# Polysketch attention into a SwiGLU block: key sums of the third batch in steps, two matmul groups one unit later, one subtraction on another engine

## The chip, the cores and the metric

One core of a Trainium2 chip runs the whole program in one launch. The metric is the device time of that launch in microseconds, given as the median of the runs shown. Each core has TensorE (PE; its weight loads are PEld), VectorE (DVE), ScalarE (ACT), GpSimd (POOL) and SyncE (SP); instructions of one engine run in the order in which they are issued, and engines wait for each other by semaphores. DMA transfers are issued from the queues of SP, ACT and POOL.

## The reference

```python
def phi(x):                                   # x: (4, 4, 1088, 32), S1 and S2: (8, 32)
    a = einsum('rd,bhsd->bhsr', S1, x)
    b = einsum('rd,bhsd->bhsr', S2, x)
    return einsum('bhsi,bhsj->bhsij', a, b).reshape(..., 64)
q_p, k_p = phi(q), phi(k)
kv  = einsum('bhsf,bhsd->bhfd', k_p, v)
z   = sum(k_p, axis=2)
num = einsum('bhsf,bhfd->bhsd', q_p, kv)
den = einsum('bhsf,bhf->bhs', q_p, z)[..., None] + 1e-06
x   = (num / den) as (4352 tokens, 128)
out = (silu(x @ w_gate) * (x @ w_val)) @ w_out    # 128 -> 1536 -> 128
```

Batches are numbered 0 to 3 in the code; "the third batch" of the title is the last one, `b = 3`.

## The kernel before

The SwiGLU block is most of the work. Its 4352 tokens are cut into blocks: three for batch 0 (of 384, 320 and 384 tokens) and seven of up to 480 tokens for the rest (`line` holds these seven, blocks 3 to 9). The hidden width of 1536 is cut into 12 chunks of 128. The last phase of the kernel is one loop over `y` from 0 to 83 (lines 1396 to 1411): unit `y` is chunk `y % 12` of block `3 + y // 12`.

One unit (`fine_unit`, line 1003) makes six matmuls (line 1012): gate and value product, each of three matmuls on parts of the numbers (x1, x0, xd against three parts of the weights). ACT takes the silu (line 1017), DVE multiplies (line 1026) and writes the hidden chunk h into a slot of `hbuf`. Each unit's two products take a pair of PSUM banks, of which there are three; the pair is free again when line 1026 has read it. Each h is cut into three parts too (`cut_hidden`, line 966): ACT makes h1 (line 983), DVE makes h0 one unit later (line 990), and hd, the sum of h and h1 (which has the opposite sign), is made either on DVE (line 994) or, for the chunks of blocks 3 to 5 but for three and for every second chunk of blocks 6 to 8, by two DMAs: SP copies h into hd (line 980), and POOL then issues a DMA that adds h1 into hd (line 985). Six units later, after `fine_unit`, `down` (line 1072) makes the three matmuls of that chunk with `w_out` (line 1084), with h1, h0 and hd in this order. Tiles for these parts come from a free list (`h_more`, line 915): rooms of earlier tiles join it from a given unit on.

The parts of a block's tokens are made ahead by `cut_tokens` (line 877): x1 on ACT (line 885) and the difference xd (line 894), then x0 on DVE (line 888), then its scaling on ACT (line 902). The loop at lines 1391 to 1395 says in which units each step is issued; block 5 (m = 2), used from unit 24, has units 20, 21 and 22.

The attention of batches 1 to 3 runs between these units. It is a Python generator (`attentions`, line 624) that stops at each `yield`. After a unit, `parts_of` (line 1409) lets it go on by one step, in the units that its condition names. A `yield "pe"` marks a group of matmuls; the generator stays there until `group()` is called, ahead of the units in `GROUPS` (line 1387). For batches 2 and 3 the groups are: keys with values and key sums (line 397, then line 724 through `value_sums`), query sketches (line 351), and numerators (line 798). The groups of batch 3 are the ones ahead of units 27, 29 and 44.

Behind the numerators of batch 2 (group ahead of unit 20) the key features of batch 3 are made on DVE, in four products of 3, 2, 2 and 2 chunks of the tile `late` (`features`, line 714; the operation is line 386): the generator stops behind the first, the third and the fourth. Then POOL adds the nine chunks up into `zs`, in five additions (`feature_sums`, line 552, the operation is line 556):

```python
def last():
    add(s[:, 0, :], s[:, 0, :], s[:, 1, :])
    add(s[:, 0, :], s[:, 0, :], rows[:, 8, :])
return s[:, 0, :], [
    lambda: add(s, rows[:, 0:2, :], rows[:, 2:4, :]),
    lambda: add(s, s, rows[:, 4:6, :]),
    lambda: add(s, s, rows[:, 6:8, :]),
    last,
]
```

`value_sums` (line 721) reads `zs` on TensorE into the bank that holds the keys with values; DVE folds that into the query weights (lines 610 to 617) and turns the rest (line 734), and SP sends six small copies of it (`spread`, line 748), one per unit.

Of the kernel before, what the change touches and what calls it, by code (L numbers as in the profile page):

```python
# [19 lines left out]
def kernel(  # L20
# [28 lines left out]
    nc = tc.nc  # L49
# [72 lines left out]
    def pair(keep=None):  # L122

        i = min((i for i in (0, 4, 6) if i not in held), key=lambda i: max(used[i], used[i + 1]))
        touch(i, i + 1)
        if keep is not None:
            held.add(i)
            kept[keep] = i
        return PS[:, i : i + 2, :]
# [3 lines left out]
    def let_go(keep):  # L133
        i = kept.pop(keep)
        held.discard(i)
        touch(i, i + 1)
# [17 lines left out]
    qld = const.tile([P, 4 * NC, Dh], FP32, tag="qld", name="qld", bufs=1)  # L154
    vld = const.tile([P, H, NC, Dh], FP32, tag="vld", name="vld", bufs=1)
    kT = const.tile([P, NC, 4, 32], FP32, tag="kT", name="kT", bufs=1)
    qT = const.tile([P, 4 * NC, 32], FP32, tag="qT", name="qT", bufs=1)
# [160 lines left out]
    late = const.tile([P, NL - NX1, BW], FP32, tag="late", name="late", bufs=1)  # L318
# [40 lines left out]
    def key_products(ps, c0, c1):  # L359

        for c in range(c0, c1):
            for a in (0, 2):
                nc.tensor.matmul(  # L363
                    ps[32 * a : 32 * a + 64, 64 * (c - c0) : 64 * (c - c0) + 64],
                    kT[:, c, a : a + 2, :].rearrange("p a t -> p (a t)"),
                    s12[:].rearrange("p h t r -> p (h t r)"),
                    start=True,
                    stop=True,
                )
# [206 lines left out]
    def turn_keys(b):  # L576

        for c in kpieces:
            turn_k(*c)
            if c[1] == NC and b + 1 < B:  # L580
                load_k(b + 1)
            yield

    def turn_queries(b):

        for x0, x1 in ((0, 4 * kpieces[0][1]), (4 * kpieces[0][1], 4 * NC)):
            nc.vector.transpose(out=qT[:, x0:x1, :], in_=qld[:, x0:x1, :])
            if x1 == 4 * NC and b + 1 < B:
                load_q(b + 1)
            yield  # L590
# [33 lines left out]
    def attentions():  # L624

        yield from turn_keys(1)
        kp = pair("keys")
        for i, c in enumerate(kpieces):  # L630
            key_products(kp[:, i, :], *c)
        ka = apool.tile([P, NC * H, R], FP32, tag="kas", name="kas")

        def sketch(ps, i):
            c0, c1 = kpieces[i]
            return ps[:, i, 0 : 64 * (c1 - c0)].rearrange("p (x t r) -> p x t r", t=2, r=R)

        for i, (c0, c1) in enumerate(kpieces):
            nc.scalar.copy(ka[:, H * c0 : H * c1, :], sketch(kp, i)[:, :, 0, :])
        yield from turn_queries(1)  # L640
        phk = apool.tile([P, NC, H, R, R], FP32, tag="phk", name="phk")
        for n, (i, c0, c1) in enumerate(((0, 0, 3), (0, 3, 5), (1, 5, 7), (1, 7, 9))):
            first = H * (c0 - kpieces[i][0])
            kb = sketch(kp, i)[:, first : first + H * (c1 - c0), 1, :]
            key_features(phk, (ka[:, H * c0 : H * c1, :], kb), c0, c1)
            if n == 0:
                zs, sums = feature_sums(phk)
            else:
                sums.pop(0)()
            if n == 3:  # L650
                let_go("keys")
            if n % 3 != 1:
                yield
        sums.pop(0)()
        yield from turn_keys(2)
        kvz = pair("values")
        key_values(kvz[:, 0, 0:F], phk, 0, NC)
        kab, copies = sketched(pair(), key_products, 2, "kab2")
        run_copies(copies, 2)
        value_sums(kvz[:, 0, :], zs)  # L660
        fold(kvz[:, 0, :])
        spread = spread_out(1, kvz[:, 0, :])
        let_go("values")
        yield
        qab, copies = sketched(pair(), query_sketches, 3, "qab")
        run_copies(copies, 2)
        yield
        yield from query_step(1, qab)
        numerators(1, spread)
        yield "first"  # L670

        phk = apool.tile([P, NC, H, R, R], FP32, tag="phk", name="phk")
        yield from features(phk, kab)
        zs, sums = feature_sums(phk)
        for f in sums:
            f()
        yield from turn_keys(3)
        yield from turn_queries(2)
        for b in (2, 3):
            yield "pe"  # L680
            kv = bank("g2")
            key_values(kv[:, 0:F], phk, 0, NC)
            if b == 2:
                kab, copies = sketched(pair(), key_products, 2, "kab2")
                run_copies(copies, 2)
            value_sums(kv, zs)
            fold(kv)
            spread = spread_out(b, kv)
            yield
            yield "pe"  # L690
            qab, copies = sketched(pair(), query_sketches, 3, "qab")
            run_copies(copies, 2)
            yield
            if b == 2:
                yield from turn_queries(3)
            yield from query_step(b, qab)
            yield "pe"
            numerators(b, spread)
            yield
            if b == 2:  # L700
                phk = late[:].rearrange("p s (n h i j) -> p (s n) h i j", h=1, i=R, j=R)
                phk = phk.rearrange("p (c h) o i j -> p c (h o) i j", h=H)
                yield from features(phk, kab)
                zs, sums = feature_sums(phk)
                for f in sums:
                    f()
                yield

    def run_copies(copies, n):
        for f, *args in copies[:n]:  # L710
# [3 lines left out]
    def features(phk, kab):  # L714
        for n, (c0, c1) in enumerate(((0, 3), (3, 5), (5, 7), (7, 9))):
            x = slice(H * c0, H * c1)
            key_features(phk, (kab[:, 0, x, :], kab[:, 1, x, :]), c0, c1)
            if n % 3 != 1:
                yield
# [157 lines left out]
    def cut_tokens(i, engine=nc.gpsimd):  # L877

        t0, n = blocks[i]
        x = xcols(t0, n)  # L880
        x1, x0, xd = x_parts[i] = [
            apool.tile([P, WB], F32R, tag=tag, name=name, bufs=2)
            for tag, name in (("qb", "x1"), ("dT", "x0"), ("rd", "xd"))
        ]
        nc.scalar.activation(x1[:, 0:n], x, AF.Copy, scale=CUT)

        def low():
            nc.vector.scalar_tensor_tensor(
                out=x0[:, 0:n], in0=whole(x1[:, 0:n]), scalar=-PART, in1=x,
                op0=ALU.mult, op1=ALU.add,  # L890
            )

        def difference():
            engine.tensor_tensor(
                out=xd[:, 0:n], in0=x, in1=whole(x1[:, 0:n]), op=ALU.subtract
            )

        difference()
        yield
        low()  # L900
        yield
        nc.scalar.activation(x0[:, 0:n], whole(x0[:, 0:n]), AF.Copy, scale=LIFT)  # L902
# [11 lines left out]
    h_sets, h_free = {}, []  # L914
    h_more = [
        (1, (("wg", 3), ("wv", 3), ("soon", 3), ("extra", 4), ("xT0", 2))), (6, (("kT", 2), ("kld", 2))),
        (9, (("qld", 2),)), (30, (("vld", 2), ("qT", 2), ("late", 4))),
    ]
    before, behind = {}, {}

# [272 lines left out]
    n = steps[0][1]  # L1193
    pss = query_products(*steps[0], "ab")
    qbs = [query_copy(n, *ps) for ps in pss]
    phk = apool.tile([P, NC, H, R, R], FP32, tag="phk", name="phk")
# [47 lines left out]
    def parts_of(n):  # L1244

        for _ in range(n):
            if ahead[0] not in ("pe", "end"):
                ahead[0] = next(att, "end")
# [135 lines left out]
    slots[:] = [flat[:, WB * k : WB * k + WB] for k in range((NH - NL - NX0) * BW // WB)]  # L1384

    END = len(line) * NCH
    GROUPS = (4, 6, 20, 27, 29, 44)
    LONGER = (18, 42)
    LAG = 6

    token_steps = {}
    for m, i in enumerate(line[1:], 1):
        gen = cut_tokens(i, nc.gpsimd if m < 3 else nc.vector)
        for at in {1: (3, 8, 9), 2: (20, 21, 22), 3: (28, 32, 33), 4: (44, 45, 46)}.get(m, range(NCH * m - 10, NCH * m - 7)):
            token_steps.setdefault(at, []).append(gen)
    for y in range(END):
        if y == NCH * (len(line) - 1):
            rest = apool.tile([P, 6, BW], FP32, tag="phk", name="rest")
            slots += [rest[:, k, :] for k in range(6)]
        if y in GROUPS:  # L1400
            group()
        fine_unit(line[y // NCH], y % NCH, y, mixed=(y == 0))
        if going:
            going.pop(0)()
        for _ in range(2):

            if len(todo) > min(LAG + (y in LONGER), END - y + 1):
                down(y)
        parts_of(y < 30 or y % 2 == 0 or y % 4 == 1)
        for gen in token_steps.get(y, ()):  # L1410
            next(gen, None)
    ps = wide("a")[:, 0, 0:D]
# [42 lines left out]
```

## Time and profile before

| what | value |
|---|---|
| median of 3 runs | 275.98 us (275.47 to 276.18) |
| the profiled execution: its own time | 275.28 us |
| its span, first to last instruction | 273.6 us (1.7 us lie around it) |
| PE busy | 263.9 us, 96% of the span |
| DVE busy | 228.8 us, 84% |
| ACT busy | 147.4 us, 54% |
| POOL busy | 87.4 us, 32% |
| chain that ended last, by engine | PE 85%, DVE 8%, POOL 2%, DMA 2% |
| mean granted TensorE clock | 0.992 |

How to read it: all times in the views are microseconds from the start of the span. A line of the timeline gives the start, the length, the engine, the line of the kernel, the operation and output <- inputs; in brackets stands how long the engine sat idle before it, and what released it. "DMA share" is the busy share of the core's 16 DMA engines.

### The profile page before, as it was taken

Reading aid. Unit: us, or ns where it says so; the run is one execution under the profiler, and the core shown is the slowest. Engines: PE = TensorE matmul, PEld = TensorE weight load, DVE = VectorE, ACT = ScalarE, POOL = GpSimd, SP = SyncE. Lnnn points to the kernel's source line nnn. Section 1 sums busy time; section 2 is a strip of 40 time slices with the busy share of each in tenths; the row PEclk is TensorE's granted clock in tenths of the full one; section 3 lists DMA queues with packets and bytes.
Section 4 is the critical chain, followed back from the end, with each engine's and each line's share of the span. In section 5 each row is a group of like instructions: output and inputs, shape, how many; then the busy total and the mean of one; then the engine's idle time right before and its main releaser. Section 6 shows DMA issues by size and latency. Waiting matters only on the chain.

```text
span 273.6 us, 5967 instructions
## 1 busy us (share of the span) xinstructions
PE 263.9 (96%) x2228; PEld 208.4 (76%) x2228; DVE 228.8 (84%) x441; ACT 147.4 (54%) x309; POOL 87.4 (32%) x113
## 2 busy tenths in 40 slices
PE   8899999999999999999997699999999999999995
PEld 7545566667786787888786588887888888889994
DVE  3997988989798988999699369997979888878861
ACT  3468665462545557856554165654766646565430
POOL 3314422149020692424448612322122212212000
PEclk9999999999999999999999799999999999999999
DMA  6583196222231048999999538886555775476111
GB/s 194 171 226 90 40 270 201 65 100 59 63 96 21 1 103 228 215 223 267 220 217 216 114 97 180 188 174 162 132 116 123 154 152 130 110 164 123 17 21 29
DMA packets 39677, 37.42 MB, mean 137 GB/s; under 512 B 21344, under 2 KB 37728, under 8 KB 39648
## 3 DMA queue, kind: packets, MB, share of 16 engines
q1 hardware_dynamic: 31648, 24.83, 31.4%
q0 software_dynamic: 6768, 11.55, 24.8%
q10 hardware_dynamic: 1232, 0.66, 0.9%
q8 instruction: 17, 0.28, 0.4%
q14 instruction: 12, 0.10, 0.1%
HBM read 11.41 MB, written 2.23 MB: 50 GB/s over the span
## 4 chain that ended last, share of the span: by engine, by line
PE 85%; DVE 8%; POOL 2%; DMA 2%; issue 1%; ACT 1%; SPq 0%; DVEq 0%; POOLq 0%
PE PS L1012 39%; PE PS L1084 16%; PE PS L1043 11%; PE PS L1089 7%; POOL zs L556 2%; PE PS L351 2%; PE PS L243 2%; DMA out_dram<-o 2%; PE PS L798 2%; PE PS L363 1%; PE PS L1105 1%; DVE hbuf L1026 1%; DVE room L869 1%; PE PS L397 1%; PE PS L506 1%
## 5 line engine op out<-in xcount | busy, mean ns | idle before, releaser
L1017 ACT ACTIVATE sg<-PS 128x480 f32<-128x480 f32 (+1 forms) x90 | 50.0, 556 | 70.2 <-PE PS L1012 70.2
L1026 DVE SCALAR_TENSOR_TENSOR hbuf<-PS,sg 128x480 f32<-128x480 f32 (+2 forms) x84 | 52.0, 622 | 15.1 <-ACT sg L1017 13.5
L1012 PE MATMUL PS<-x,graw 128*128 128x480 f32 (+1 forms) x117 | 46.3, 396 | 0.0
L1012 PE MATMUL PS<-xd,wd 128*128 128x480 f32 (+1 forms) x90 | 33.8, 375 | 0.0
L1012 PE MATMUL PS<-x,wb 128*128 128x480 f32 (+1 forms) x90 | 33.6, 373 | 0.0
L1012 PE MATMUL PS<-x,w 128*128 128x480 f32 (+1 forms) x90 | 33.6, 373 | 0.0
L1012 PE MATMUL PS<-xd,graw 128*128 128x480 f32 (+1 forms) x69 | 25.8, 374 | 0.0
L1012 PEld LDWEIGHTS PS<-x,graw 128*128 128x128 f32 x117 | 22.1, 189 | 4.7 <-issue 0.9
L1012 PE MATMUL PS<-x,gphq 128*128 128x480 f32 (+1 forms) x63 | 24.4, 388 | 0.0
L1043 PE MATMUL PS<-xT,wg 128*128 128x384 f32 (+1 forms) x60 | 23.5, 473 | 0.1
L1043 PE MATMUL PS<-xT,wv 128*128 128x384 f32 (+1 forms) x60 | 23.2, 468 | 0.3 <-DVE wv L288 0.3
L1012 PEld LDWEIGHTS PS<-x,w 128*128 128x128 f32 x90 | 17.0, 189 | 2.4
L1012 PEld LDWEIGHTS PS<-x,wb 128*128 128x128 f32 x90 | 17.0, 189 | 2.1
L1012 PEld LDWEIGHTS PS<-xd,wd 128*128 128x128 f32 x90 | 17.0, 189 | 2.1
L1047 ACT ACTIVATE sg<-PS 128x384 f32<-128x384 f32 (+1 forms) x24 | 11.2, 468 | 13.2 <-PE PS L1043 12.4
L1089 PE MATMUL PS<-hbuf,wo 128*128 128x384 f32 (+3 forms) x48 | 18.2, 475 | 0.0
L1043 PEld LDWEIGHTS PS<-xT,wv 128*128 128x128 f32 x60 | 11.2, 190 | 7.4 <-DVE hbuf L1058 0.8
L1043 PEld LDWEIGHTS PS<-xT,wg 128*128 128x128 f32 x60 | 10.9, 190 | 7.7 <-issue 1.1
L1012 PEld LDWEIGHTS PS<-xd,graw 128*128 128x128 f32 x69 | 13.1, 190 | 2.6 <-issue 0.6
L1012 PEld LDWEIGHTS PS<-x,gphq 128*128 128x128 f32 x63 | 12.0, 190 | 2.5 <-ACT x L902 0.3
L1084 PE MATMUL PS<-hextra,dparts 128*128 128x480 f32 (+1 forms) x37 | 11.7, 389 | 0.0
L1089 PEld LDWEIGHTS PS<-hbuf,wo 128*128 128x128 f32 x48 | 8.8, 189 | 2.7
(260 smaller groups left out, 592.6 us busy)
## 6 DMA issues: line engine op xcount, KB each, us to landing
kld<-in_k_dram SPq DMA_DIRECT2D x4, 544.0 KB, 4.0
hextra<-hbuf SPq DMA_DIRECT2D x9, 240.0 KB, 2.7
hwv<-hbuf SPq DMA_DIRECT2D x8, 240.0 KB, 3.0
qld<-in_q_dram SPq DMA_DIRECT2D x3, 544.0 KB, 5.4
raw<-in_moe_w_out_dram SPq DMA_DIRECT2D x4, 384.0 KB, 4.8
hwg<-hbuf SPq DMA_DIRECT2D x6, 240.0 KB, 3.6
hwg<-hwg POOLq DMA_DIRECT2D x6, 240.0 KB, 3.9
hwv<-hwv POOLq DMA_DIRECT2D x6, 240.0 KB, 4.1
```

Source lines behind the costliest of these rows:

```text
L243: nc.tensor.matmul(ps[0:32, 0:w], warm[:, 0:32], warm[:, 0:w], start=True, stop=True)
L351: nc.tensor.matmul(ps[32 * a : 32 * a + 32, 96 * (c - c0) : 96 * (c - c0) + 96], qT[:, 4 * c + a, :], s123[:, a : a + H, :, :].rearrange(" ...
L363: nc.tensor.matmul(ps[32 * a : 32 * a + 64, 64 * (c - c0) : 64 * (c - c0) + 64], kT[:, c, a : a + 2, :].rearrange("p a t -> p (a t)"), s12 ...
L556: add = lambda o, a, b: nc.gpsimd.tensor_tensor(out=o, in0=a, in1=b, op=ALU.add)
L798: nc.tensor.matmul(num[a // 2][32 * h : 32 * h + 32, a % 2, 0 : 32 * n], kvr[r, s, g, :], phT[r, s, g, 0:n, :], start=(g == 0), stop=(g == 1),
L1012: nc.tensor.matmul(ps[:, k], w_parts[id((wg, wv)[k]), j // 3][t][:, j % 3, :], xs[t], start=(t == 0), stop=(t == 1),)
L1017: nc.scalar.activation(sg, ps[:, 0], AF.Silu, scale=PART)
L1026: nc.vector.scalar_tensor_tensor(out=hj[:, a:b], in0=ps[:, 1, a:b], scalar=scale, in1=sg[:, a:b], op0=ALU.mult, op1=ALU.mult,)
L1043: nc.tensor.matmul(o[:, 0:n], w[:, j, :], xcols(t0, n), start=True, stop=True)
L1047: nc.scalar.activation(sg[:, 0:n], g[:, 0:n], AF.Silu)
L1084: nc.tensor.matmul(acc[i][:, 0:n], w, h, start=(first and t == 0), stop=(last and t == 2))
L1089: nc.tensor.matmul(acc[i][:, 0:n], wo[:, j, :], hidden[i, j][:, 0:n], start=first, stop=last)
```

## The change

The five additions for batch 3 are issued in two steps between the feature products: none behind the first product, two behind the third, and the rest (the third and the two of `last`) behind the fourth. (For `n = 0` the slice is `sums[-2:0]`, which is empty.) Before, all five came one generator step behind the fourth product. The groups ahead of units 27 and 29 move to units 28 and 30. The tiles that these groups read (`vld`, `qT`, `late`) join the free list from unit 31 instead of 30. The difference xd of block 5 is made by DVE instead of POOL. From unit 30 on, the generator goes on in four of five units instead of three of four.

```diff
@@ attentions, b == 2
-                yield from features(phk, kab)
                 zs, sums = feature_sums(phk)
-                for f in sums:
-                    f()
-                yield
+                for n, _ in enumerate(features(phk, kab)):
+                    for f in sums[2 * n - 2 : 2 * n]:
+                        f()
+                    yield
@@ h_more
-        (9, (("qld", 2),)), (30, (("vld", 2), ("qT", 2), ("late", 4))),
+        (9, (("qld", 2),)), (31, (("vld", 2), ("qT", 2), ("late", 4))),
@@ the last loop
-    GROUPS = (4, 6, 20, 27, 29, 44)
+    GROUPS = (4, 6, 20, 28, 30, 44)
...
-        gen = cut_tokens(i, nc.gpsimd if m < 3 else nc.vector)
+        gen = cut_tokens(i, nc.gpsimd if m == 1 else nc.vector)
...
-        parts_of(y < 30 or y % 2 == 0 or y % 4 == 1)
+        parts_of(y < 30 or y % 5 > 0)
```

On POOL's queue the order around the change is, before: add-DMA of hwv, xd (line 894), add-DMAs of hsoon, hextra and hxT, the five additions, add-DMAs of hkld and hwg. After: add-DMA of hwv, add-DMA of hsoon, two additions, add-DMA of hextra, three additions, add-DMAs of hxT, hkld and hwg.

## The prediction
> **What bounds the kernel now.** The page comes first: TensorE is busy for 96% of the span, and only in one place does its clock digit fall (slice 23, from 150.5 us on). The other engines matter where they make it wait.
>
> ```profile
> PE 263.9 (96%) x2228; PEld 208.4 (76%) x2228; DVE 228.8 (84%) x441; ACT 147.4 (54%) x309; POOL 87.4 (32%) x113
> PEclk9999999999999999999999799999999999999999
> ```
>
> The list of waits then gives TensorE's one long wait, the key sums of batch 3:
>
> ```profile
> PE PS L724 <- POOL zs L556: 3.7, 1, 3.7
> ```
>
> TensorE's timeline around it shows the price. Columns: start, length, instruction, idle time before it.
>
> ```profile
> 147.08 0.81 PE L1084 MATMUL PS<-hsoon,dparts 128*128 128x480 f32 x3
> 147.82 1.21 PE L397 MATMUL PS<-late,vld 128*32 128x64 f32 x72
> 152.76 0.32 PE L724 MATMUL PS<-zs,ones 128*32 128x64 f32 x8 [3.72 <-POOL zs L556]
> 153.01 0.77 PE L1012 MATMUL PS<-x,gphq 128*128 128x480 f32 x1
> ...
> 156.63 0.38 PE L1012 MATMUL PS<-x,gphq 128*128 128x480 f32 x1
> ```
>
> Unit 27 runs from 153.01 to 156.63, 3.62 us; a unit elsewhere takes 1.96 (units 30 to 33 begin at 162.35, 164.29, 166.27 and 168.22 in the same timeline). The busy times by stretch say why: behind the wait the granted clock is half.
>
> ```profile
> 149.60:153.03 3.43, 0.27 (x9) 0.18 (x9) 0.94 (x2) 0.00 (x0) 3.27 (x4) 1.00 0.34 119
> 153.03:156.44 3.41, 3.41 (x13) 2.88 (x10) 1.99 (x6) 1.06 (x2) 1.79 (x3) 0.50 0.72 124
> ```
>
> (Columns: length; busy PE, PEld, DVE, ACT, POOL; clock; DMA share.) So the place costs 3.72 + (3.62 - 1.96) = **5.38 us**.
>
> POOL's timeline says what comes ahead of the sums, and so what the change moves past them:
>
> ```profile
> 138.29 0.86 POOL L985 DMA_DIRECT2D hwv<-hwv  x1 [2.01 <-ACT hsoon L983]
> 138.86 1.55 POOL L894 TENSOR_TENSOR xd<-xT,x 128x480 fp32r<-128x480 f32 x1
> 142.58 0.88 POOL L985 DMA_DIRECT2D hsoon<-hsoon  x1 [2.18 <-ACT x L902]
> 144.72 0.86 POOL L985 DMA_DIRECT2D hextra<-hextra  x1 [1.26 <-DMA hextra<-hbuf]
> 145.60 0.87 POOL L985 DMA_DIRECT2D hxT<-hextra  x1
> 146.16 1.63 POOL L556 TENSOR_TENSOR zs<-late 128x512 f32<-128x512 f32 x1
> 147.87 3.23 POOL L556 TENSOR_TENSOR zs<-zs,late 128x512 f32<-128x512 f32 x2
> 151.18 0.72 POOL L556 TENSOR_TENSOR zs<-zs 128x256 f32<-128x256 f32 x1
> 151.98 0.72 POOL L556 TENSOR_TENSOR zs<-zs,late 128x256 f32<-128x256 f32 x1
> ```
>
> The hsoon line names ACT, but nothing of line 902 is needed there. SP issues its copy at 136.14 and that lands 5.9 us later (the view of DMA issues), at 142.04; hextra, issued at 138.19 with 6.0 us, starts 0.53 us after its landing too. So hsoon waits for its copy, and the change leaves that time alone.
>
> **Part by part, on the clock of this profile.**
>
> *The sums earlier.* POOL goes on 0.57 us behind a DMA issue (138.29 to 138.86). The first two additions then begin at 143.15; their features are done by 139.8 (below). An addition takes 1.6, with 0.1 between: 143.15 and 144.86, ended at 146.45. The hextra DMA starts there instead of at 144.72. At 147.02 the third addition follows, at 148.68 and 149.48 the two of 0.72, and at 150.15 the hxT DMA instead of at 145.60. The sums are ready at 150.2 instead of 152.7.
>
> *The group one unit later.* Unit 26 ends at 147.73; about 0.1 of that goes, since unit 24's third matmul sat at 142.22 behind line 902's end at 142.17, which comes earlier. Without a wait unit 27 begins at 147.65, its six matmuls take 1.30, and it ends at 149.6. The keys and values take 1.22 (147.82 to 149.04 = 152.76 - 3.72), so the sums are wanted at 150.9, 0.7 us after they are ready. **The wait goes, and with it the half clock**: -5.38 and -0.1.
>
> *What is late next.* hd of the two chunks whose DMAs now stand behind additions. Third matmuls of `down` start 1.30 + 2 x 0.217 = 1.73 behind a unit's start. In unit 27 that is hextra's hd: wanted at 149.4, issued at 146.45. In unit 28 it is hxT's: the group (1.56, as 147.73 to 153.01 less the wait) ends at 151.2, so wanted at 152.95, issued at 150.15. How long such a DMA takes is known from rows of the same 240 KB: hextra 3.9 us, hkld at 152.65 3.2 us. That lands hextra at 149.65 to 150.35 (a wait of 0.3 to 1.0) and hxT at 153.35 to 154.05 (0.4 to 1.1 in all, since the first wait pushes the second unit back). I take **+0.8**, between the two rows. Bounds: the shortest such landing here is 3.1 (hwv at 156.03), which leaves 0.3; the longest is 8.2 (hqld at 131.75, at a DMA share of 1.07 from 130 to 142), which is the slow rival. A wait of 1 us leaves the clock alone as far as this trace shows, which has a fall only behind 3.72.
>
> *xd on VectorE.* One subtraction more on DVE, 0.66 by the row of line 894 at 159.12 (0.57 to the next instruction), one of 1.55 less on POOL. While POOL's ran, two feature products on DVE took 2.93; the one after it 0.68. So DVE gains 1.7, pays 0.57, and x0 (line 888) begins at 139.8 instead of 140.88. Off TensorE's path but for the 0.1 counted above. If the cover were gone it would cost its 0.57.
>
> *DVE under the additions.* With an addition running, lines 990 and 994 take 1.72 instead of 0.65, line 1026, which reads PSUM, still 0.65. The same now befalls lines 990 of hxT, hkT and hqld and 994 of hqld, one per addition. Laid out so, line 1026 of unit 26 comes at 149.9, as it does now. Its banks are wanted by unit 29 at about 154: 3.5 us hide it; without that, 1.1 per addition.
>
> *Queries, spread, steps.* Line 351 (1.69) and its ACT copies move by a unit and are paid as before. With the skipped steps moved, the last transpose for the numerators comes in unit 39 instead of 38, and the six spread copies on SP's queue start in unit 28 instead of 27. Both are wanted ahead of unit 44, five units (9.8 us) later: nothing. The out stores behind the spread copies and the tiles free from unit 31 are waited for by nobody sooner: nothing. Each could cost at most one unit, 1.96.
>
> **Sum:** 275.28 - 5.38 - 0.1 + 0.8 = 270.6 for the profiled execution. The median lies 0.7 above that execution, so the forecast is **271.3 us**.
>
> **Rivals.**
>
> *No wait is left*: DMA landings of 2.9 us or less, with the DMA engines emptier than now. 275.98 - 5.48 = 270.5. For it: behind 146.4 the hextra DMA runs alone on POOL's queue, where the page's rows have it beside hxT. Against it: none of this size landed under 3.1 here. The Trainium skill (DMA: Bandwidth & Descriptors, Anatomy of one DMA — SWDGE (gpsimd) path) fits such a DMA as 2.0 us plus bytes over 436e3 per us, an estimate of 2.6 us for 240 KB; by that this rival would be the outcome, and no row here is that short.
>
> *The queue stays full*: landings of about 6 (5.6 for hwv at 138.29, 6.4 for hwg at 135.42). hextra lands at 152.45, a wait of 3.05 in unit 27; hxT at 156.15, 3.2 behind 152.95 in all. 275.98 - 5.48 + 3.2 = 273.7. For it: the DMA share is 1.06 from 144 to 150. Against it: it is that full because hextra and hxT themselves run there.
>
> *The sums still come last*, so that the change doesn't do what it says: the additions get longer, with more of DVE's operations on two SBUF inputs among them. With 0.5 more for each of the five (half of the 1.1 that DVE loses to one) hextra goes out at 147.45, a wait of 1.6 in unit 27; the sums are ready at 152.7, 0.2 late again at line 724; and hxT, out at 152.65, lands 3.25 late in all: 273.8. For it: DVE is busy without a gap from 137 to 150.5. Against it: that holds now too, and none took over 1.63.
>
> *Slower*: hextra's hd takes 6.7 us or more. Then unit 27 waits 3.7 us at `down`, as line 724 does now, the clock falls behind it as now (1.66), and the rest is lost too. With the 8.2 of the slowest row: 154.65, a wait of 5.25, plus 1.66: 275.98 - 5.48 + 6.9 = 277.4. For it: that one row. Against it: it was the fourth such DMA issued within 3.3 us, beside out stores, whose last is issued at 139.42 and, at 5.1, lands by 144.6.
>
> **Chances.** Forecast (0.3 to 1.5 us of wait left) 0.60, no wait 0.15, full queue 0.13, sums last 0.06, slower 0.06. Within 0.3%, or 0.8 us, which is about what a measurement of this kernel can tell from no change, lies only the upper end of the full queue: 0.03. So faster 0.91, same 0.03, slower 0.06. The range takes in no wait (270.5, less half of the 0.7 that the runs spread, and a little) and the full queue: 269.9 to 273.7.
>
> **What would show it.** Right: line 724 without a wait; no 0.50 clock behind it; lines 1084 of hextra in unit 27 and of hxT in unit 28 with waits of 0.3 to 1 for a DMA; POOL's sums ended near 150; feature products of 0.68 and xd of 0.66 on DVE. Wrong: a wait at line 724, L985 landings over 4.5 us, a half clock anywhere from 145 to 165, or a new wait of TensorE on line 1026 or ahead of the numerators.

## The result, and the profile after

| | before | after |
|---|---|---|
| median | 276.08 us (275.47 to 277.42, 4 runs) | 273.33 us (272.83 to 274.41, 4 runs) |
| ratio, 95% interval | | 0.9899 (0.9852 to 0.9947) |
| profiled execution, its span | 275.28, 273.6 us | 274.41, 272.4 us |
| mean granted clock of it | 0.992 | 0.994 |

The change is faster by about 1%, inside the range and on the forecast side, but 2 us short of the 271.3 that was forecast: the median fell by 2.75 us, where 4.7 was forecast. The profiled execution of after is the slowest of its four; the others show a clock of 0.999 to 1.000 and 272.83 to 273.56 us.

The page of the profile after still has TensorE busy almost throughout, and still one dip of the clock, one slice later (slice 24):

```profile
PE 264.4 (97%) x2228; PEld 208.2 (76%) x2228; DVE 229.2 (84%) x442; ACT 148.3 (54%) x309; POOL 86.4 (32%) x112
PEclk9999999999999999999999979999999999999999
```

The wait at line 724 is gone from the list of TensorE's waits; half as long a wait, for hxT's add-DMA, is now the longest:

```profile
PE PS L1084 <- DMA hxT<-hextra: 1.9, 1, 1.9
```

TensorE's timeline of after, from unit 26's `down` to the start of unit 29 (columns as before):

```profile
147.22 1.05 PE L1084 MATMUL PS<-hsoon,dparts 128*128 128x480 f32 x3
148.10 0.37 PE L1012 MATMUL PS<-x,gphq 128*128 128x480 f32 x1
...
149.39 1.16 PE L1084 MATMUL PS<-hextra,dparts 128*128 128x480 f32 x3
150.48 1.21 PE L397 MATMUL PS<-late,vld 128*32 128x64 f32 x72
151.51 0.29 PE L724 MATMUL PS<-zs,ones 128*32 128x64 f32 x8
...
155.59 0.49 PE L1084 MATMUL PS<-hxT,dparts 128*128 128x480 f32 x1 [1.86 <-DMA hxT<-hextra]
155.92 0.38 PE L1012 MATMUL PS<-x,gphq 128*128 128x480 f32 x1
```

Line 724 follows line 397 without a pause. The three matmuls of `down` take 0.81 without a pause (hsoon's in the kernel before); here hsoon's took 1.05, hextra's 1.16, and hxT's third one sat for 1.86. POOL's timeline shows why hxT's part was late: its DMA stands behind all five additions.

```profile
142.90 0.86 POOL L985 DMA_DIRECT2D hsoon<-hsoon  x1 [1.49 <-PE PS L1012]
143.46 1.61 POOL L556 TENSOR_TENSOR zs<-late 128x512 f32<-128x512 f32 x1
145.15 1.61 POOL L556 TENSOR_TENSOR zs<-zs,late 128x512 f32<-128x512 f32 x1
146.70 0.87 POOL L985 DMA_DIRECT2D hextra<-hextra  x1
147.31 1.58 POOL L556 TENSOR_TENSOR zs<-zs,late 128x512 f32<-128x512 f32 x1
148.97 1.04 POOL L556 TENSOR_TENSOR zs<-zs 128x256 f32<-128x256 f32 x1
150.09 1.03 POOL L556 TENSOR_TENSOR zs<-zs,late 128x256 f32<-128x256 f32 x1
151.07 0.86 POOL L985 DMA_DIRECT2D hxT<-hextra  x1
```

The view of DMA issues gives this DMA 4.5 us to landing, so it landed at 155.57, just ahead of the matmul that waited for it:

```profile
hxT<-hextra POOLq DMA_DIRECT2D x1, 240.0 KB, 4.5
```

And the busy times by stretch (length; busy PE, PEld, DVE, ACT, POOL; clock; DMA share; GB/s) show that behind the 1.86 us the clock fell again:

```profile
153.21:156.62 3.41, 1.55 (x8) 1.03 (x7) 2.79 (x5) 1.09 (x3) 1.23 (x2) 1.00 1.09 193
156.62:160.03 3.41, 3.41 (x34) 2.53 (x36) 1.83 (x3) 1.06 (x2) 0.99 (x2) 0.50 0.79 184
```

From unit 29's start to unit 30's first matmul it takes 5.20 (155.92 to 161.12). The kernel before took 3.66 for a unit and the same group of matmuls (line 351) at full clock (156.63 to 160.29). That makes 1.54 us for the clock.

### The profile page after: what moved, and what is told of

Its sections match the earlier page's. It is cut to its first block, busy times and chain, and to the rows that moved or that the text cites. A ratio compares the mean times of both kernels' runs of the same rounds, so it can differ in the third digit from the quotient of the medians.

```text
span 272.4 us, 5968 instructions
## 1 busy us (share of the span) xinstructions
PE 264.4 (97%) x2228; PEld 208.2 (76%) x2228; DVE 229.2 (84%) x442; ACT 148.3 (54%) x309; POOL 86.4 (32%) x112
## 4 chain that ended last, share of the span: by engine, by line
PE 83%; DVE 8%; DMA 3%; POOL 2%; issue 1%; ACT 1%; SPq 0%; POOLq 0%; DVEq 0%; ACTq 0%
PE PS L1012 40%; PE PS L1084 17%; PE PS L1043 10%; PE PS L1089 7%; PE PS L351 2%; POOL zs L556 2%; DMA hxT<-hextra 2%; PE PS L798 2%; DMA kld<-in_k_dram 2%; PE PS L363 1%; DVE phk L386 1%; PE PS L1105 1%; DVE room L869 1%; PE PS L397 1%; PE PS L506 1%
```

## The experiments

Each kernel ran 6 to 12 times, and its ratio is against the kernel before on the same chip, which had medians of 276.85, 276.49 and 276.58 us in the three groups that shared a chip (the first four, the next four, the last).

**The changed kernel again**, with no edit.

> The changed kernel once more, for its spread and its granted clock. Theory: what is left is a wait of TensorE of about 1.9 us for hxT's add-DMA in unit 28, and the half clock behind it falls in some executions only, since 1.9 us is shorter than the 3.7 us that always lost it: executions with a mean clock of 1.000 take 272.6 to 273.4 us, those with 0.994 about 1.5 us more. Rival: the wait always costs the clock; then all executions show 0.994 and lie near 274.4, and the spread has another cause.

Measured: 272.84 us (272.55 to 275.64), ratio 0.9887 (0.9852 to 0.9922). In its own profile TensorE waits 1.59 us for hxT and the clock stays at 1.000. Two of ten executions have a clock of 0.994: 274.60 and 275.64 us, against a median of 272.8 for the other eight. With the four above, 3 of 14 lost the clock. So the clock falls in some executions only, as the theory says, and the rival (always) is out. It doesn't explain all of the spread: one execution took 274.33 at a clock of 1.000, and it has no profile.

**One addition a unit**: the additions go one behind unit 21, one behind 22, three behind 23.

```diff
                 for n, _ in enumerate(features(phk, kab)):
-                    for f in sums[2 * n - 2 : 2 * n]:
+                    for f in sums[max(n - 1, 0) : n]:
                         f()
                     yield
+                for f in sums[2:]:
+                    f()
+                yield
```

> The changed kernel with one addition behind unit 21, one behind unit 22 and three behind unit 23, so that the add-DMAs of hextra and hxT are each issued one addition earlier or more. Theory (the wait left comes from where these two DMAs stand among the additions on POOL's queue): hextra's goes out near 145, hxT's near 147, both waits at line 1084 go, the sums are ready near 150.7 to 151.2 and cost TensorE 0 to 0.5 us at line 724; 270.5 to 271.2 us, clock 1.000. Rival (the DMA engines are full, the landing is late whatever the order): hxT lands only near 154 to 155 again, TensorE waits there, 272.5 to 273.5 us.

Measured: 271.40 us (270.99 to 272.31), ratio 0.9821 (0.9783 to 0.986). POOL issues the add-DMAs of hextra and hxT earlier:

```profile
145.14 0.87 POOL L985 DMA_DIRECT2D hextra<-hextra  x1
146.99 1.17 POOL L985 DMA_DIRECT2D hxT<-hextra  x1
```

TensorE's timeline has no wait at line 1084 in units 27 and 28; what is left is a short one at the key sums (line 724, which is line 727 in this kernel):

```profile
151.76 0.32 PE L727 MATMUL PS<-zs,ones 128*32 128x64 f32 x8 [0.49 <-POOL zs L556]
...
153.63 0.60 PE L1084 MATMUL PS<-hxT,dparts 128*128 128x480 f32 x2
```

The order on POOL's queue is the cause of that wait, as the theory says: the same additions and the same DMAs in another order, 1.4 us less than the whole change. The time is 0.2 above the expected span.

**Only the groups later**: sums in one piece and xd on POOL as before.

```diff
-    GROUPS = (4, 6, 20, 27, 29, 44)
+    GROUPS = (4, 6, 20, 28, 30, 44)
```

(with the free list from unit 31 and `parts_of(y < 30 or y % 5 > 0)`, as in the change.)

> The kernel before with only the two groups one unit later (and the tiles from unit 31, the changed skip of steps); the five additions in one piece and xd on POOL as before. Theory: the add-DMAs of hextra and hxT stay ahead of the additions, so no wait at line 1084; the sums are ready at 152.7 and wanted at 150.9, a wait of about 1.8 us at line 724: 272.0 to 272.6 us, no slower than the whole change, or 1.5 more where the clock falls. Rival (the steps of the sums are what brings the gain): most of the wait at line 724 stays, about 3 us or more, with the half clock behind it: 274 us or more.

Measured: 273.97 us (273.24 to 274.34), ratio 0.9903 (0.9865 to 0.9941), not told apart from the whole change (0.9887; the intervals overlap, and the medians differ by 1.1 us). Its profile, with the clock at 1.000:

```profile
143.22 0.48 PE L1012 MATMUL PS<-xd,gphq 128*128 128x480 f32 x1 [0.49 <-POOL xd L894]
...
154.22 0.32 PE L724 MATMUL PS<-zs,ones 128*32 128x64 f32 x8 [2.02 <-POOL zs L556]
```

It has 2.02 us at line 724 instead of the 1.8 expected, and no wait at line 1084 in units 27 and 28. The expected 272.0 to 272.6 was missed, and the record shows two causes beside that 0.2: xd, behind hwv's late copy on POOL's queue, came 0.49 late, and three of six executions lost the clock (0.992 to 0.994; these have a median of 274.3, the others 273.3).

**The change without xd on DVE**:

```diff
-        gen = cut_tokens(i, nc.gpsimd if m == 1 else nc.vector)
+        gen = cut_tokens(i, nc.gpsimd if m < 3 else nc.vector)
```

> The change without its third part: xd of block 5 on POOL again. Theory: the first addition is held up by the hsoon copy's landing, not by xd, which ends 2 us sooner; so the waits at line 1084 stay as in the changed kernel, and the time too, within 0.4 us. Rival (xd on POOL slows the feature products that the additions need, 2.9 us for two instead of 1.3): the additions come 1 us or more later and so does hxT's DMA; 1 us or more slower than the changed kernel.

Measured: 273.26 us (272.02 to 275.52), ratio 0.9891 (0.9857 to 0.9926), against 0.9887 with xd on DVE; the medians are 0.4 us apart, which is the edge of what the theory allowed. POOL's first addition begins at 143.91 instead of 143.63 (the changed kernel run again), hxT's DMA at 151.53 instead of 151.27. The waits at line 1084 are there, of 0.31 us for hextra and 1.20 for hxT. So the third part of the change brings nothing that can be measured here.

**hd of the two chunks on DVE**: no add-DMA for hextra and hxT.

```diff
-        carried = i in line[:3] and (i, j) not in [(line[2], x) for x in (0, 3, 7)] or i in line[3:-1] and j % 2
+        carried = i in line[:3] and (i, j) not in [(line[1], 9), (line[1], 10)] + [(line[2], x) for x in (0, 3, 7)] or i in line[3:-1] and j % 2
```

> The changed kernel, but hd of chunks 9 and 10 of block 4 (hextra's and hxT's, used in units 27 and 28) is made by DVE at line 994, without the SP copy and without the add-DMA of POOL. Theory (the wait left is those two add-DMAs' landing): TensorE no longer waits at line 1084 in units 27 and 28, the sums end near 149.5 and are in time; 270.6 to 271.6 us at clock 1.000, if DVE's two subtractions (0.65, and up to 1.7 under an addition) stay hidden. Rival (the wait is for something that comes about in units 27 and 28 anyway, DVE's lateness or full DMA engines): a wait of over 1 us stays on line 1084 or 1012 there; 272.5 us or more.

Measured: **270.35 us** (270.03 to 271.51), ratio 0.9796 (0.9763 to 0.9828), below both kernels; no execution lost the clock. TensorE's timeline has no wait in these units:

```profile
149.12 0.81 PE L1084 MATMUL PS<-hextra,dparts 128*128 128x480 f32 x3
149.87 1.21 PE L397 MATMUL PS<-late,vld 128*32 128x64 f32 x72
150.89 0.29 PE L724 MATMUL PS<-zs,ones 128*32 128x64 f32 x8
152.52 0.38 PE L1084 MATMUL PS<-hextra,dparts 128*128 128x480 f32 x1
152.74 0.60 PE L1084 MATMUL PS<-hxT,dparts 128*128 128x480 f32 x2
```

Slightly below the expected 270.6 to 271.6, and far from the rival's 272.5. The wait was for those two DMAs, and TensorE doesn't wait for DVE's two additional subtractions (0.66 and 1.73 us).

**The first addition in POOL's gap**: features in chunks of 4, 2, 2 and 1, so that the first addition can run ahead of hsoon's DMA (the rest is as with one addition a unit).

```diff
-                for n, _ in enumerate(features(phk, kab)):
-                    for f in sums[max(n - 1, 0) : n]:
-                        f()
+                for n, _ in enumerate(features(phk, kab, (0, 4, 6, 8, 9))):
+                    sums[n]()
                     yield
-                for f in sums[2:]:
-                    f()
+                sums[3]()
                 yield
...
-    def features(phk, kab):
-        for n, (c0, c1) in enumerate(((0, 3), (3, 5), (5, 7), (7, 9))):
+    def features(phk, kab, cuts=(0, 3, 5, 7, 9)):
+        for n, (c0, c1) in enumerate(zip(cuts, cuts[1:])):
```

> Like the kernel with one addition a unit, but the features are cut into 4, 2, 2 and 1 chunks, so that the first addition can be issued behind unit 20, ahead of hsoon's add-DMA, in the time in which POOL waits for hsoon's copy. Theory: the additions end near 150, TensorE waits nowhere from unit 24 to 28; 270.5 to 271.2 us, 0.3 to 0.6 below the kernel with one addition a unit. Rival: the first addition now runs beside DVE's feature products and x0, which get 1 to 1.7 us longer; x0 is late for unit 24 (line 1012 waits there 0.5 to 1.5 us), 271.5 to 272.5 us.

Measured: 271.35 us, ratio 0.9815 (0.978 to 0.9849): no better than one addition a unit, and between the theory's span and the rival's. Its six executions spread from 269.83 to 272.61, and the profile is of the slowest. There the rival's wait is seen, for x0, and a second one, for line 1026:

```profile
PE PS L1012 <- DVE hbuf L1026: 1.0, 1, 1.0
PE PS L1012 <- ACT x L902: 0.9, 1, 0.9
```

x0's step on DVE (line 888) took 2.48 us beside the addition that ran from 140.94, and line 990 took 2.47 beside a later one. With these two waits, of 0.93 and 0.95, all six executions kept the clock (0.999 or 1.000). Whether the best execution (269.83) had no such wait can't be seen, since it has no profile; that stays open.

**Only the steps**: groups and xd as before.

```diff
-                yield from features(phk, kab)
                 zs, sums = feature_sums(phk)
-                for f in sums:
-                    f()
-                yield
+                for n, _ in enumerate(features(phk, kab)):
+                    for f in sums[2 * n - 2 : 2 * n]:
+                        f()
+                    yield
```

> The kernel before with only the additions in steps; groups ahead of units 27 and 29, xd on POOL. Theory: the sums end near 150.5 to 151.2 and are wanted at 149.0, a wait of 1.5 to 2.2 us at line 724 instead of 3.7; hextra's hd is wanted only behind it and in time, hxT's is about 0.3 to 0.8 late: 272.4 to 273.5 us, most of it without the half clock. Rival (only the later group removes the wait): 274.5 us or more, with the half clock as before.

Measured: 274.30 us (272.1 to 275.47), ratio 0.9919 (0.9891 to 0.9947). The wait is as the theory has it, 2.10 us, and hextra and hxT come in time; but 9 of 11 executions lost the clock (0.987 to 0.994), so the time lies above the expected span. The two that kept it took 272.10 and 272.63.

```profile
151.47 0.32 PE L724 MATMUL PS<-zs,ones 128*32 128x64 f32 x8 [2.10 <-POOL zs L556]
```

**Only xd on DVE.**

```diff
-        gen = cut_tokens(i, nc.gpsimd if m < 3 else nc.vector)
+        gen = cut_tokens(i, nc.gpsimd if m == 1 else nc.vector)
```

> The kernel before with only xd of block 5 on DVE. Theory: POOL's first addition is set by hsoon's copy, hextra's copy and the two add-DMAs, not by xd; the wait at line 724 stays at 3.5 to 3.9 us with the half clock behind it; within 0.6 us of the kernel before. Rival: with 1.55 us less on POOL the additions end 1 us or more sooner and the wait shrinks; 274.5 us or less against a median of before near 276.5.

Measured: 276.64 us (275.66 to 278.1), ratio 1.0017 (0.9991 to 1.0043), no difference, with a wait of 3.62 us at line 724. Its profile also has a wait of 0.87 for hwv's add-DMA in unit 25, which before's did not have. The theory holds: POOL's 1.55 us were spent while it had to wait for hsoon's copy anyway.

**hxT's DMA without followers**: hd of the two chunks behind it on DVE.

```diff
-        carried = i in line[:3] and (i, j) not in [(line[2], x) for x in (0, 3, 7)] or i in line[3:-1] and j % 2
+        carried = i in line[:3] and (i, j) not in [(line[1], 11)] + [(line[2], x) for x in (0, 1, 3, 7)] or i in line[3:-1] and j % 2
```

> The changed kernel, but hd of the two chunks behind hxT's (chunk 11 of block 4 and chunk 1 of block 5, tiles hkld and hwg) is made by DVE, so that hxT's add-DMA is not followed within 1.2 us by two more and their copies are gone. Theory (hxT lands in 4.2 to 4.5 us instead of the 3.2 to 3.9 that the prediction took, because those two share the DMA engines with it): it lands in 3.1 to 3.4 us, TensorE's wait at line 1084 in unit 28 shrinks from 1.6 to 1.9 us to 0.4 to 1.0, and the time falls by about 1 us, to 271.6 to 272.2. Rival (the landing takes over 4 us by itself): landing and wait stay, 272.6 to 273.3 us.

Measured: 273.07 us (272.48 to 274.73), ratio 0.9883 (0.9844 to 0.9922). The theory of this experiment falls, and the rival's time came out: with nothing behind it on POOL's queue until 156.56, hxT still lands 4.0 us after its issue, and TensorE waits 1.39 us.

```profile
155.45 0.49 PE L1084 MATMUL PS<-hxT,dparts 128*128 128x480 f32 x1 [1.39 <-DMA hxT<-hextra]
```

The busy times by stretch (length; PE, PEld, DVE, ACT, POOL; clock; DMA share; GB/s) show where the time goes, with the issue at 151.41:

```profile
150.00:152.00 2.00, 1.67 (x82) 1.35 (x81) 2.00 (x4) 1.06 (x2) 1.92 (x3) 1.00 0.04 8
152.00:153.00 1.00, 1.00 (x15) 0.85 (x5) 1.00 (x2) 0.41 (x1) 0.28 (x1) 1.00 0.15 27
153.00:154.00 1.00, 1.00 (x5) 0.57 (x4) 1.00 (x3) 0.65 (x2) 0.00 (x0) 1.00 1.14 198
154.00:155.00 1.00, 0.06 (x1) 0.00 (x0) 0.93 (x5) 0.71 (x2) 0.00 (x0) 1.00 0.78 252
```

In stretches of 0.3 us the same view has next to nothing on the DMA engines for 1.2 to 1.5 us after the issue; then they are full at 192 to 198 GB/s for 1.2 us (about 240 KB). Behind that comes what by its time and size is hwv's plain copy, issued by SP at 152.58; it runs until 155.0, at 327 to 358 GB/s in its main part, and only then, at 155.41, the landing shows. hextra's add-DMA in the same profile, with no such copy behind its data, landed in 3.3 us. So a part of the 4.0 may be that copy; this is not shown. The two followers are not needed for a late landing, and not enough for one: with them hxT landed in 4.2 and 4.5 us in the changed kernel, but in 3.8 in the change without xd and in 3.2 in the kernel with only the steps.

## Why the prediction was right, and which size was off

*Where the gain comes from*: right. The wait at line 724 is gone, with the half clock behind it; the sums end at 151.1 and are used at 151.5, without a pause (0.4 to spare, where 0.7 was worked out).

*Which part brings it*: the later groups alone give 0.9903 and the steps alone 0.9919; they don't add up, since both take from the same wait, and both together bring the wait at line 1084. The prediction had the group and the sums as one term and did not say that the group alone would do nearly as well.

*xd on VectorE*: right, at next to nothing (1.0017 alone, and 0.9891 without it against 0.9887 with it). Line 902's pause in unit 24 is gone, as counted. With xd on DVE it can also no longer stand on POOL behind a late add-DMA, which cost TensorE 0.49 in one profile (only the groups later); that was not foreseen.

*What is late next*: the mechanism was right, place and all (hextra in unit 27, hxT in unit 28); **the term of +0.8 was mis-sized**. By the start of hxT's third matmul it measured 2.4. That matmul started at 155.59. Unit 26 would have ended at 147.88 without hsoon's pause, and the prediction's own distance of 5.30 from there (147.65 to 152.95) gives 153.18. Of the 1.6 too little, 0.6 are the last two additions (1.04 and 1.03 instead of 0.72 each, since DVE's operations on two SBUF inputs now ran beside them), and 0.9 the landing (4.5 instead of the 3.6 that +0.8 stands for). The kernel before had a nearer row than the two that were taken: hxT's own add-DMA, issued at 145.60, took 4.5 us there too by the view of DMA issues, and with that the term would have been 1.7. What makes the landing that long stays open (see the last experiment). hsoon's pause of 0.2 in unit 26 was not in the sum; it is covered by the later wait. The 0.3 by which this profile runs late from the start (unit 24 at 142.02 instead of 141.71) is no part of the 2.4.

*"A wait of 1 us leaves the clock alone"*: the one profile with waits of 0.93 and 0.95 kept it, and so did the other five executions of that kernel (the first addition in POOL's gap). But the waits left by the change were 1.6 to 1.9 in its two profiles, and 3 of its 14 executions lost it, for 1.54 us in the one that has a profile. The forecast had no such term.

*Its own signs*: two of those named for "wrong" came out, a half clock between 145 and 165 and landings of line 985 above 4.5 us (4.8 for hsoon, 4.9 for hkld, 5.6 for hwg). The wait that the forecast left, 0.3 to 1.5 us, stands for 270.8 to 272.0; 273.33 lies above that, toward the full queue. That it is still inside the range is owed to the range taking in that rival's 273.7.

*The price of the wait before*: the profiled execution was a cheap one. Of 52 further executions of before, 46 show a clock of 0.994 or less, and 27 of these 0.988 or less; the medians are 274.8 us at 0.998 and above, 276.1 from 0.991 to 0.994, 277.1 from 0.988 down. The profile of the kernel with only xd on DVE shows what such a low clock can be. Its mean is 0.988, and around and behind its wait the clock is half for about 6.8 us, twice the 3.41 of before's profile (a value between 0.50 and 1.00 means half clock in a part of the stretch):

```profile
150.00:153.60 3.60, 0.45 (x34) 0.29 (x22) 0.00 (x0) 0.00 (x0) 3.37 (x4) 0.96 0.57 135
153.60:154.20 0.60, 0.12 (x7) 0.13 (x8) 0.00 (x0) 0.00 (x0) 0.60 (x2) 0.50 0.03 10
154.20:157.60 3.40, 3.40 (x16) 2.74 (x16) 1.71 (x6) 1.06 (x2) 1.65 (x3) 0.50 0.68 117
157.60:161.00 3.40, 3.40 (x12) 2.69 (x10) 1.28 (x3) 1.29 (x3) 0.73 (x1) 0.63 0.62 107
```

So the median pays more for the clock than the 1.66 counted, and the 0.7 that the prediction added for the median may be in part that clock. This error works for the change and the +0.8 against it; that they partly cancel is luck. With the sizes as measured (5.48 gained, 2.4 left) the sum from 275.98 would be 272.9, near the 273.33 and the 272.84; but it still prices the clock by one cheap profile, so this nearness proves little.

*The rivals*: "no wait is left" came out at the time given for it (270.5) once the two DMAs were taken away: 270.35. Its condition, landings of 2.9 us or less, was met by neither of the two DMAs in any profile. The estimate of 2.6 us from the Trainium skill (DMA: Bandwidth & Descriptors, Anatomy of one DMA — SWDGE (gpsimd) path) is not borne out here: in the changed kernel hextra took 3.3, hxT 4.2 and 4.5, and the shortest landing of these two DMAs in any profile was 3.2. "The queue stays full" has hxT's wait right in kind, but hextra, which it had 3.05 late, came 0.35 late. "The sums still come last" did not come about: the first three additions took 1.6 as before, only the last two grew. Nor did "slower".

## What to carry to other kernels

When work is moved ahead on an engine that also issues DMAs in order, count every DMA that it now stands in front of, and when that DMA's data is wanted: here splitting the work so that the DMAs go first (271.40 us), or taking the two DMAs off the queue (270.35), got what the change itself left behind (272.84). A short wait of TensorE has to be priced with the chance that the clock falls behind it, and a profile is one draw of that: look at the clock of all runs before taking a profiled stall as the typical one. And when a DMA's landing has to be priced, start from the row of that same DMA in the profile before, here 4.5 us and not 3.2 to 3.9.

## What the runs showed of the hardware

The clock falls behind shorter waits than expected, and not every time. Each kernel has one profile, the change two; the list goes by the longest wait there between units 24 and 29, and the waits of the other executions are not known. Executions with a clock of 0.994 or less:

| wait of TensorE, us | kernel | lost the clock |
|---|---|---|
| 0 | hd on DVE | 0 of 6 |
| 0.49 | one addition a unit | 0 of 6 |
| 0.95 | the first addition in POOL's gap | 0 of 6 |
| 1.20 | the change without xd | 1 of 10 |
| 1.39 | hxT without followers | 1 of 6 |
| 1.59 and 1.86 | the change | 3 of 14 |
| 2.02 | only the groups later | 3 of 6 |
| 2.10 | only the steps | 9 of 11 |
| 3.62 | only xd on DVE | 12 of 12 |
| 3.72 | before | 46 of 52 |

So even in the kernel with the 3.72 us wait the clock does not always fall, though the theory of the first experiment took it that it does. The kernels differ in more than this wait, so the shares are a trend and no rule. The half clock lasted 3.41 us in the profiles of before and of after. The Trainium skill (TensorE: Matmul & The Clock Gate, Part 1: The HAM clock gate) has a free-running window of 3413 ns, which would make it a matter of where the wait falls; the length and the share that grows with the wait agree with that. In the section Why this matters for your kernels, that page of the Trainium skill advises no gaps over about 3 us; here the clock fell behind 1.86.

An addition on POOL slows those of DVE's operations that have two SBUF inputs (lines 990 and 888: 0.65 alone, 1.65 to 2.48 beside one of 128x512, 1.19 where it overlapped only a part of one or one of 128x256), while line 1026, with one input in PSUM, stays at 0.65. The addition of 128x256 is itself slower then (1.04 instead of 0.72). An add-DMA of 240 KB that POOL issues had 1.2 to 1.5 us ahead of its data and then moved 173 to 198 GB/s (hextra's and hxT's in the kernel without followers), where the plain copy of the same size moved 327 to 358.
